# One row of an output projection on eight DMA engines, A's projection in four pieces, and eight tiny matmuls at the start

## The chip, the cores and the metric

The kernel runs on one core of one Trainium2 chip. The metric is the device time of one execution in microseconds (us). A kernel is told by the median of its runs, and two kernels are compared by runs of the same rounds on the same chip. A difference under 2% is called "same".

Some words used below: PE is the matrix engine, DVE and ACT are the vector and scalar engines, SP is the engine that issues the loads. A matmul on PE comes with a weight load, recorded apart (2328 of each in the kernel before). Sixteen DMA engines move the data; the packets that one of them moves, one behind the other, are called its stream, and the 4-byte packet with which it reports its part of a load as done is its semaphore packet. Between the packets of the loads, in the same streams, stand packets of two queues that the profile calls "instruction" (in the kernel before six of 16,384 bytes on q8, and from 1.0 us on two of 8,192 on q14); such a packet is taken to bring a block of an engine's program and is called a fetch, one of 8,192 bytes a half fetch. A stand is a time in which PE is idle in the middle of its work although it waits for no semaphore ("issue" in the profile).

## The reference

There are two attention layers with one query each, A and B. They differ only in how much of the cache they see: A the last 2048 of 8192 positions, B all.

```python
B, Sq, D = 1, 1, 576
Hq, Hkv, Sk, Dh = 32, 16, 8192, 128
W = min(4096, max(256, Sk // 4))                       # 2048, A only
q = (x @ wq).reshape(B, Sq, Hq, Dh)...                  # transposed to heads
k = jnp.repeat(k_cache[:, :, Sk - W:, :], rep, axis=1)  # B: the whole cache
v = jnp.repeat(v_cache[:, :, Sk - W:, :], rep, axis=1)
p = softmax(einsum("bhqd,bhkd->bhqk", q, k) * Dh ** -0.5)
o = einsum("bhqk,bhkd->bhqd", p, v)
return o.transpose(...).reshape(B, Sq, Hq * Dh) @ wo    # wo: 4096 x 576
out = concatenate([a, b], axis=-1)
```

The last step is what the change touches: a row of 4096 numbers times `wo`. The kernel puts 32 rows of `wo` on each of 128 partitions ("row 31" is the last of them on every partition), so the product is 32 steps of a 128-deep matmul.

## The kernel before

After five rounds of caches (one for A, four for B) the kernel loads both `wo` into the buffers of the K and V cache as these come free, then multiplies. A's product is in two pieces of 288 columns (64 matmuls), B's in four of 144 (128 matmuls).

```python
OUTS = [2, 4]
# ... (setup, loads of K and V, transposes, scores, softmax, sums over V)

    def load_wo(P, lo, n, off, res):
        load(slots[:, off:off + n * DM], lambda: wos[P].rearrange("(p j) n -> p (j n)", p=128)[:, lo * DM:(lo + n) * DM],
             res, "wo%d_%d" % (P, lo))

    def wo_part(P, lo, n, off, res):
        def mm(pe):
            for jj in range(lo, lo + n):
                w = DM // OUTS[P]
                for j in range(OUTS[P]):
                    o = off + (jj - lo) * DM + j % 2 * (DM // 2) + j // 2 * w
                    at = jj + j % 2 * 31
                    ins = pe.matmul(ktps[P + j // 2][32 * j:32 * j + 32, 0:w], lhsT=opj[:, P, at:at + 32],
                                    rhs=slots[:, o:o + w], start=(jj == 0), stop=(jj == HQ - 1))
            return ins
        add("pe", mm, reads=[("opj", P)] + res, writes=[("bank", P + k) for k in range(P + 1)])

# ...
    wo_loads = [
        (0, 0, 32, 0, [("k", 0), ("k", 1, 0)]),
        (1, 0, 21, WQ_W, [("k", 1, 1)]),
        (1, 21, 7, 2 * SLOT, [("v", 0), ("v", 1)]),
        (1, 28, 3, 2 * SLOT + 7 * DM, [("w", 0)]),
        (1, 31, 1, 2 * SLOT + 10 * DM, [("w", 1)])]
    for P, lo, n, off, res in wo_loads:
        load_wo(P, lo, n, off, res)
    combine([NG - 1])          # B's last four matmuls that gather the heads
    o_columns(1)
    for P in range(2):
        for Q, lo, n, off, res in wo_loads:
            if Q == P:
                wo_part(P, lo, n, off, res)
        finish_out(P)
```

## Time and profile before

| what | before |
|---|---|
| time, median (lowest to highest) | 245.43 us (245.33 to 245.59), 3 runs |
| span of the profiled execution | 243.8 us |
| A's product starts / ends | 232.7 / 236.8 us |
| B's first part starts, after its weights | 238.29 us |
| last load landed / last matmul ended | 241.94 / 242.26 us |
| 16 KiB instruction fetches (queue q8), start | 38.03, 50.50, 65.08, 71.18, 236.06, 240.13 us |

The profile's page is read from the engine shares to the DMA slices and queues, then the chain of work that ended last, then the timeline of the tail. Those lines, and how packets were put to streams, are shown in the prediction. "Last landing" is the last semaphore packet of the last load plus the time until its update is seen (0.44 us here).

### The profile page before, as it was taken

The page shows a single profiled execution, that of the slowest core. Times are in us where ns is not written, and L with a number is a line of the kernel's source. Part 1 is how long each engine was busy: PE and PEld are TensorE (multiplying, and loading weights), DVE is VectorE, ACT ScalarE, POOL GpSimd, SP SyncE. Part 2 cuts the span into 40 slices and gives each one's busy share as a digit, 9 for nine tenths or more (in the row PEclk, how much of TensorE's full clock was granted, in tenths as well). Part 3 has the DMA queues.
Part 4 walks back from the last instruction along what each step waited for, and adds up shares of the span by engine and source line. Part 5 has one row for each costly group of instructions (what it writes and reads, how often), then busy time and mean ns, then how long its engine had stood idle before and what let it go on. Part 6 is the DMA issues. An engine that isn't in the chain of part 4 may idle for free. (4 is left out here: it accounts for less than half of the span.)

```text
span 243.8 us, 5220 instructions
## 1 busy us (share of the span) xinstructions
PE 164.1 (67%) x2328; PEld 119.3 (49%) x2328; DVE 88.3 (36%) x152; ACT 92.9 (38%) x96; POOL 6.8 (3%) x34
## 2 busy tenths in 40 slices
PE   0060739984387995393999472999458699746864
PEld 0020239762236773233978231987233677535753
DVE  0100126874207454203455222456321355532120
ACT  2000016876006686101677400678600387630000
POOL 6001000000000000000000000000000000000000
PEclk9996557999569999566799959799956799955899
DMA  8999999999999999899999999999989999989994
GB/s 323 452 454 396 430 430 427 425 425 430 446 427 426 489 398 462 371 430 436 495 399 462 403 409 430 430 489 419 452 382 436 436 489 398 484 376 411 422 405 177
DMA packets 4112, 102.88 MB, mean 422 GB/s; under 512 B 516, under 2 KB 648, under 8 KB 904
## 3 DMA queue, kind: packets, MB, share of 16 engines
q1 hardware_dynamic: 4040, 102.76, 98.3%
q8 instruction: 6, 0.10, 0.2%
q10 hardware_dynamic: 64, 0.00, 0.0%
q14 instruction: 2, 0.02, 0.0%
HBM read 102.76 MB, written 0.00 MB: 422 GB/s over the span
## 5 line engine op out<-in xcount | busy, mean ns | idle before, releaser
L510 ACT ACTIVATE kt<-ktps 128x1024 bf16<-128x1024 bf16 x80 | 79.4, 1038 | 86.9 <-PE ktps L500 86.9
L500 PE MATMUL ktps<-ident,slots 128*128 128x128 bf16 x1280 | 85.9, 231 | 18.9 <-PEq L214 18.2
L500 PEld LDWEIGHTS ktps<-ident,slots 128*128 128x128 bf16 x1280 | 79.9, 104 | 34.3 <-issue 34.3
L513 DVE COPY kt<-ktps 128x1024 bf16<-128x1024 bf16 x80 | 60.8, 770 | 53.3 <-PE ktps L500 53.3
L592 PE MATMUL opsum<-slots,ptm 128*32 128x512 bf16 x320 | 27.1, 511 | 12.4 <-PEq L214 12.4
L525 PE MATMUL sacc<-kt,qst 128*32 128x512 bf16 x320 | 25.4, 392 | 2.2 <-PEq L214 2.2
L592 PEld LDWEIGHTS opsum<-slots,ptm 128*32 128x32 bf16 x320 | 13.1, 123 | 25.1 <-issue 22.9
L563 PE MATMUL misc<-ident,psb 128*128 128x128 bf16 x40 | 5.1, 307 | 15.8 <-PEq L214 15.8
L610 DVE TENSOR_TENSOR vtmp<-opsum,maskV 128x512 f32<-128x512 f32 x4 | 2.8, 692 | 32.3 <-PE opsum L592 32.3
L551 ACT ACTIVATE psb<-sacc,stat 128x2048 bf16<-128x2048 f32 x5 | 9.8, 1967 | 9.7 <-DVE stat L540 9.7
L563 PEld LDWEIGHTS misc<-ident,psb 128*128 128x128 bf16 x40 | 3.9, 138 | 18.3 <-issue 18.3
L570 DVE TENSOR_TENSOR ptm<-misc,maskP 128x1024 bf16<-128x1024 bf16 x5 | 3.5, 692 | 16.4 <-PE misc L563 16.4
L525 PEld LDWEIGHTS sacc<-kt,qst 128*32 128x32 bf16 x320 | 5.0, 94 | 8.2 <-issue 4.6
L695 PE MATMUL ktps<-slots,opj 128*32 128x144 bf16 (+1 forms) x192 | 6.8, 247 | 2.7 <-DMA slots<-in_B_wo_dram 2.7
L707 ACT ACTIVATE outsb<-ktps 64x144 bf16<-64x144 f32 x1 | 0.3, 288 | 21.5 <-PE ktps L695 21.5
L460 PE MATMUL turned<-slots,xpad 128*32 128x512 bf16 x36 | 4.0, 631 | 6.4 <-DMA slots<-in_B_wq_dram 6.4
L475 DVE CAST qcol<-misc 128x32 bf16<-128x32 f32 x2 | 0.6, 300 | 19.8 <-PE misc L471 19.8
L695 PEld LDWEIGHTS ktps<-slots,opj 128*32 128x32 bf16 x192 | 5.2, 97 | 4.1 <-DMA slots<-in_B_wo_dram 3.6
L460 PE MATMUL opsum<-slots,xpad 128*32 128x512 bf16 x36 | 3.5, 559 | 5.2 <-DMA slots<-in_A_wq_dram 5.2
L485 POOL COPY qst<-qcol 128x32 bf16<-128x32 bf16 x8 | 1.7, 213 | 153.1 <-PE sacc L525 153.1
L441 PE MATMUL misc<-xnine,twice 16*128 16x18 bf16 x4 | 0.3, 171 | 8.0 <-DMA xnine<-in_B_x_dram 8.0
L466 ACT ACTIVATE qrow<-opsum 128x512 bf16<-128x512 f32 x1 | 0.6, 598 | 12.8 <-PE opsum L460 12.8
(77 smaller groups left out, 57.0 us busy)
## 6 DMA issues: line engine op xcount, KB each, us to landing
slots<-in_B_k_cache_dram SPq DMA_DIRECT2D x8, 4096.0 KB
slots<-in_A_k_cache_dram SPq DMA_DIRECT2D x4, 2048.0 KB
slots<-in_A_v_cache_dram SPq DMA_DIRECT2D x4, 2048.0 KB
slots<-in_B_wq_dram SPq DMA_DIRECT2D x1, 4608.0 KB, 23.1
slots<-in_A_wo_dram SPq DMA_DIRECT2D x1, 4608.0 KB, 20.0
slots<-in_A_wq_dram SPq DMA_DIRECT2D x1, 3072.0 KB, 12.6
slots<-in_B_wo_dram SPq DMA_DIRECT2D x1, 3024.0 KB, 27.1
slots<-in_A_wq_dram SPq DMA_DIRECT2D x1, 1536.0 KB, 6.2
```

Source lines behind the costliest of these rows:

```text
L460: ins = pe.matmul((turned if P else opsum)[32 * j:32 * j + 32, :], lhsT=xpad[:, P, u, :], rhs=slots[:, o:o + 512], start=(u == 0), stop=(u ...
L485: return pool.tensor_copy(dst, src)
L500: ins = pe.matmul(ktps_bf[q][:, t * 128:(t + 1) * 128], lhsT=slots[:, o:o + 128], rhs=ident[:, :], start=True, stop=True, is_transpose=True)
L510: add("act", lambda act, src=src, dst=dst: act.activation(dst, src, ACT.Copy), reads=[("bank", q)], writes=[("kt", u % NKT, q)], tag="e%d% ...
L513: add("dve", lambda dve, src=src, dst=dst: dve.tensor_copy(dst, src), reads=[("bank", q)], writes=[("kt", u % NKT, q)], tag="e%d%d" % (u, q))
L525: ins = pe.matmul(sacc[32 * j:32 * j + 32, :], lhsT=qst[:, o:o + 32], rhs=rhs, start=(u == 0 and e == 0), stop=True, skip_group_check=True)
L551: return act.activation(dst, src, ACT.Exp, bias=st(C_NB + g), scale=SCALE, accum_out=st(C_L + g))
L563: ins = pe.matmul(dst[:, t * 128:(t + 1) * 128], lhsT=psb[:, o:o + 128], rhs=ident[:, :], start=True, stop=True, is_transpose=True)
L570: return dve.tensor_tensor(ptm[:, c * 1024:(c + 1) * 1024].rearrange("p (t y) -> p t y", t=8), dst.rearrange("p (t y) -> p t y", t=8), mas ...
L592: ins = pe.matmul(opsum[64 * j + 32 * x:64 * j + 32 * x + 32, :], lhsT=ptm[:, o:o + 32], rhs=v[:, at[0], at[1], :, :, b:b + 128], start=(n ...
L610: add("dve", lambda dve: dve.tensor_tensor(vtmp[:, :, :], src, by, ALU.mult), reads=[B_O, w], writes=["vtmp"], tag="keep")
L695: ins = pe.matmul(ktps[P + j // 2][32 * j:32 * j + 32, 0:w], lhsT=opj[:, P, at:at + 32], rhs=slots[:, o:o + w], start=(jj == 0), stop=(jj ...
```

## The change

The streams of the sixteen DMA engines don't end together (their last semaphores came at 239.52 to 241.50 us in the kernel before), and the last load waits for the latest. The intent, as far as the change shows it, is to move a little work from the late streams to the early ones. A's row 31 is taken off the load that all sixteen carry and is loaded by eight engines only (four rows on each of partitions 0 to 31). The product is rearranged accordingly (sixteen matmuls that are 32 deep, from a weight tile `opjR`), A's result is made in four pieces as B's is, and eight tiny matmuls are put at the start of PE's program.

```diff
+    def warm_up(pe):
+        for k in range(8):
+            ins = pe.matmul(misc[0:32, 400:401], lhsT=ident[:, 0:32], rhs=ident[:, 0:1], start=True, stop=True)
+        return ins
+    add("pe", warm_up, reads=["ident"], writes=[B_M])
 ... (cut: opjR is allocated and zeroed)
+    def wo_row(pe, P, weights, jj, row, start, stop):
+        for j in range(4):                                   # A too: four pieces of 144 columns
+            w, o, at = DM // 4, j % 2 * (DM // 2) + j // 2 * (DM // 4), jj + j % 2 * 31
+            ins = pe.matmul(ktps[2 * P + j // 2][32 * j:32 * j + 32, 0:w], lhsT=weights[:, at:at + 32],
+                            rhs=row[:, o:o + w], start=start, stop=stop)
+        return ins
+    def last_column():
+        for j in range(4):
+            add("dve", lambda dve, j=j: dve.tensor_copy(opjR[:, 31 + j:32 + j], wsum[32 * j:32 * j + 32, 303:304]), ...)
+    def load_last():
+        for i in range(4):
+            def src(i=i):
+                return wos[0].rearrange("(j e i r) n -> r i e j n", j=4, e=8, i=4)[31, i]
+            dst = bass.AP(tensor=slots, offset=(4 * SLOT) * i + 31 * DM, ap=[[4 * 4 * SLOT, 8], [DM, 4], [1, DM]])
+            add("sp", lambda sp, dst=dst, src=src: sp.dma_start(dst, src()), writes=[("last", i)], dma="last", ...)
+    def wo_last():
+        def mm(pe):
+            for j in range(4):
+                ins = wo_row(pe, 0, opjR[:, :], j, slots[0:32, (31 + j) * DM:(32 + j) * DM], False, j == 3)
+            return ins
+        add("pe", mm, ...)
 ... (cut: finish_out makes both results in two halves, one by DVE and one by ACT)
     wo_loads = [
-        (0, 0, 32, 0, [("k", 0), ("k", 1, 0)]),
-        (1, 0, 21, WQ_W, [("k", 1, 1)]),
+        (0, 0, 31, 0, [("k", 0), ("k", 1, 0)]),
+        (1, 0, 21, 35 * DM, [("k", 1, 1)]),
 ...
         load_wo(P, lo, n, off, res)
+        if P == 0:
+            load_last()
```

More of the change, by code (lines that the diff above doesn't have):

```diff
@@ L21 @@
 WQ_W = 18432
-OUTS = [2, 4]
 class Op:
@@ L338, in bass_concat_heads__sliding_block_cached__gqa_block_cached__decode_kernel @@
     accs = nc.alloc_sbuf_tensor("accs", [128, NG, DH], F32)
+    opjR = nc.alloc_sbuf_tensor("opjR", [32, 96], BF16)
     opj = nc.alloc_sbuf_tensor("opj", [128, 2, 96], BF16)
@@ L373, in setup @@
     def setup(pool):
-        for t in (ident, twice, xpad, selq, warm, identf, pick, pickB, qst):
+        for t in (ident, twice, opjR, xpad, selq, warm, identf, pick, pickB, qst):
             pool.memset(t[:], 0.0)
@@ L377, in setup @@
         return pool.memset(opj[:], 0.0)
-    add("pool", setup, writes=["ident", "twice0", ("xpad", 0), ("xpad", 1), "selq", "ones", "warm", "identf", "pick", "pickB",
+    add("pool", setup, writes=["ident", "twice0", "opjR0", ("xpad", 0), ("xpad", 1), "selq", "ones", "warm", "identf", "pick", "pickB",
                                ("qst", 0), ("qst", 1), ("opj", 0), ("opj", 1)])
@@ L690, in mm @@
             for jj in range(lo, lo + n):
-                w = DM // OUTS[P]
-                for j in range(OUTS[P]):
-                    o = off + (jj - lo) * DM + j % 2 * (DM // 2) + j // 2 * w
-                    at = jj + j % 2 * 31
-                    ins = pe.matmul(ktps[P + j // 2][32 * j:32 * j + 32, 0:w], lhsT=opj[:, P, at:at + 32],
-                                    rhs=slots[:, o:o + w], start=(jj == 0), stop=(jj == HQ - 1))
-            return ins
-        add("pe", mm, reads=[("opj", P)] + res, writes=[("bank", P + k) for k in range(P + 1)])
+                ins = wo_row(pe, P, opj[:, P, :], jj, slots[:, off + (jj - lo) * DM:off + (jj - lo + 1) * DM],
+                             jj == 0, P == 1 and jj == HQ - 1)
@@ new lines, in mm @@
+            return ins
+        add("pe", mm, reads=[("opj", P)] + res, writes=[("bank", 2 * P), ("bank", 2 * P + 1)])
+    def wo_row(pe, P, weights, jj, row, start, stop):
[6 more added lines that the diff above has]
+        for j in range(4):
+            add("dve", lambda dve, j=j: dve.tensor_copy(opjR[:, 31 + j:32 + j], wsum[32 * j:32 * j + 32, 303:304]),
+                reads=[B_W, "opjR0"], writes=[("opjR", j)])
@@ new lines, in load_last @@
+    def load_last():
[3 more added lines that the diff above has]
+            dst = bass.AP(tensor=slots, offset=(4 * SLOT) * i + 31 * DM, ap=[[4 * 4 * SLOT, 8], [DM, 4], [1, DM]])
+            add("sp", lambda sp, dst=dst, src=src: sp.dma_start(dst, src()), writes=[("last", i)], dma="last",
+                after=[("k", 1, 0), ("k", 1, 1)])
+    def wo_last():
[3 more added lines that the diff above has]
+            return ins
+        add("pe", mm, reads=[("opjR", j) for j in range(4)] + [("last", j) for j in range(4)], writes=[("bank", 0), ("bank", 1)])
@@ L702, in finish_out @@
     def finish_out(P):
-        w = DM // OUTS[P]
-        for k, name in enumerate(("dve", "act")[0:P + 1]):
-            dst, src = outsb[0:64, P, k * w:(k + 1) * w], ktps[P + k][64 * k:64 * k + 64, 0:w]
+        w = DM // 4
+        for k, name in enumerate(("dve", "act")):
+            dst, src = outsb[0:64, P, k * w:(k + 1) * w], ktps[2 * P + k][64 * k:64 * k + 64, 0:w]
             add(name, lambda eng, k=k, dst=dst, src=src:
                 eng.activation(dst, src, ACT.Copy) if k else eng.tensor_copy(dst, src),
-                reads=[("bank", P + k)], writes=[("outsb", P, k)]).key = ("outsb", P)
+                reads=[("bank", 2 * P + k)], writes=[("outsb", P, k)]).key = ("outsb", P)
@@ L709, in finish_out @@
         add("sp", lambda sp: sp.dma_start(out[0, 0:1, P * DM:(P + 1) * DM].rearrange("o (j n) -> (o j) n", j=2),
                                           outsb[31:33, P, :]),
-            reads=[("outsb", P, k) for k in range(P + 1)], writes=[("out", P)], dma="out%d" % P)
+            reads=[("outsb", P, 0), ("outsb", P, 1)], writes=[("out", P)], dma="out%d" % P)
     WQ = [(4 * SLOT - WQ_W, [("v", 2)]), (SLOT, [("k", 1, 0), ("k", 1, 1), ("v", 0)])]
@@ L772, in bass_concat_heads__sliding_block_cached__gqa_block_cached__decode_kernel @@
             o_columns(0)
+            last_column()
         v_sums(g)
@@ L789, in bass_concat_heads__sliding_block_cached__gqa_block_cached__decode_kernel @@
                 wo_part(P, lo, n, off, res)
+        if P == 0:
+            wo_last()
         finish_out(P)
```

## The prediction

> **What bounds the kernel now.** I read the page's engine shares first, then the slices of DMA and the queues, then the chain of waits at the end, then the timeline of the last 15 us, and last the trace's single records of DMA packets.
>
> The page of the kernel before (engine shares, DMA rows of the 40 slices, queues, bytes):
>
> ```profile
> PE 164.1 (67%) x2328; PEld 119.3 (49%) x2328; DVE 88.3 (36%) x152; ACT 92.9 (38%) x96; POOL 6.8 (3%) x34
> ...
> DMA  8999999999999999899999999999989999989994
> ...
> q1 hardware_dynamic: 4040, 102.76, 98.3%
> q8 instruction: 6, 0.10, 0.2%
> ...
> q14 instruction: 2, 0.02, 0.0%
> HBM read 102.76 MB, written 0.00 MB: 422 GB/s over the span
> ```
>
> No compute engine is above 67%, while the DMA engines are at 8 or 9 tenths in every slice but the last. The loads (q1) alone fill 98.3% of sixteen engines' span. So the kernel is a stream of 102.76 MB with a short tail, and only two things can move the end: fewer or better spread bytes, and what follows the last byte. The two "instruction" queues fetch the engines' own programs through the same DMA engines; they look negligible at 0.2%, and they are what this change is about.
>
> The chain of waits, its end (start us, us, what):
>
> ```profile
> 226.53 4.20 PE opsum L592 x61
> 230.73 0.02 issue
> 230.75 0.33 SPq L398
> 231.08 0.04 issue
> 231.12 10.45 DMA slots<-in_B_wo_dram
> 241.57 0.04 issue
> 241.62 0.64 PE ktps L695 x16
> 242.26 0.02 issue
> 242.28 0.30 DVE outsb L707
> ```
>
> The transfer of 10.45 us is not slow: it holds 432 KB and queues behind loads issued earlier (A's wo at 210.80, B's at 211.18 and 231.1). After the last landing come only 16 matmuls, one eviction and the store, about 2 us that the change does not touch.
>
> The timeline, output products (start us, us, what):
>
> ```profile
> 232.84 3.97 PE L695 MATMUL ktps<-slots,opj 128*32 128x288 bf16 x62
> ...
> 236.85 0.45 DVE L707 CAST outsb<-ktps 64x288 bf16<-64x288 f32 x1 [3.62 <-PE ktps L695]
> ...
> 238.29 1.50 PE L695 MATMUL ktps<-slots,opj 128*32 128x144 bf16 x84 [1.48 <-DMA slots<-in_B_wo_dram]
> 240.59 0.62 PE L695 MATMUL ktps<-slots,opj 128*32 128x144 bf16 x28 [0.81 <-DMA slots<-in_B_wo_dram]
> ```
>
> A's product ends at 236.8 and PE then waits for B's weights until 238.29: A's product is off the path, with 1.5 us to spare.
>
> The packet records settle the rest. Within one DMA engine the next packet starts 3 or 4 ns before the one before it ends, so all sixteen engines' streams can be followed from 1.0 us to their end. No stream has a gap. They do not end together: the 4-byte semaphore packets of the last load (B's row 31) come at 239.52 to 240.08 us on nine streams, 240.26 and 240.76 on two, and 241.14, 241.26, 241.30, 241.37 and 241.50 on five. Those seven streams are exactly those that carried an instruction fetch: the five have a 16,384-byte packet (at 38.03, 50.50, 65.08, 71.18 and 236.06 us, 1.02 to 1.07 us each, and the load packet after it is longer too, 1.15 us instead of 0.61 after the first), the two an 8,192-byte packet. The sixth 16,384-byte packet, at 240.13, follows no running stream: it fell on an engine that was done, and cost nothing. The kernel ends with the slowest of the five, although the mean of the sixteen semaphores is 240.4, about 1.1 us earlier.
>
> [...]
>
> **The change, part by part.**
>
> 1. *A's load of 31 rows instead of 32 on 128 partitions.* Each engine moves eight packets of 35,712 bytes instead of 36,864. A 36,864-byte packet takes 1.366 us (seven in 219.07 to 228.63), so a packet saves 1.366 x 1152/36864 = 0.043 us and each of the 16 engines 0.34 us.
> 2. *Row 31 as four DMAs of 8 x 4 rows.* Engines 0 to 7 get 16 packets of 1152 bytes and four semaphores each. A 1152-byte packet took 0.051 us in the tail, a semaphore 0.009: 0.82 + 0.04 = 0.85 us. Net: engines 0 to 7 become 0.85 - 0.34 = 0.51 us longer, engines 8 to 15 0.34 us shorter.
> 3. *A's product in four pieces.* 124 + 16 matmuls of 144 columns instead of 64 of 288. The 84 that B ran back to back took 1.50 us, 0.018 each: 140 x 0.018 = 2.5 us against 4.1 now, done near 235.3. Its eviction is split over two engines. All that lies in the slack before 238.29: worth nothing. The 16 matmuls of row 31 wait for loads that stand directly behind A's in the queue and land near 231, before PE starts on them.
> 4. *Four copies of one column on DVE* after A's cast at 226.57: DVE idles 4.0 us before 230.76, so nothing. Bank 3, now also B's, was last read at 233.0, long before B starts. Four more issues on SP come at 211, when the stream has 9 us of V queued.
> 5. *Eight tiny matmuls at the start and 76 more in the tail.* At two instructions each PE's program grows by 168[...]. A further fetch comes in the tail[...]. About 1.07 us on one engine. On a stream that would end at 240.1 it gives 241.2 at most before the shifts of step 2, so it need not be the last.
>
> Sum, if the fetches lie on engines 8 to 15: the last semaphore moves from 241.50 to 241.16; engines 0 to 7 end by 240.08 + 0.51 = 240.6, or 240.8 with the half fetch at 240.26. The end moves by -0.34 us: 245.43 - 0.34 = 245.1.
>
> **The rivals.**
>
> *One of the five late streams is among engines 0 to 7.* Then it gains 0.51 us and ends at 241.65 to 242.0: the time becomes 245.6 to 245.9. For it: nothing in the trace names the engines; if blocks 2 to 6 went to engines 2 to 6 everything seen would look the same. Against it: the change puts work on engines 0 to 7 on purpose, which makes sense only if the late ones are the others, and the two streams that stored A's result[...] have no 16 KiB fetch, only one half fetch.
>
> *The eighth block spoils it.* If the new fetch falls on a stream that already carries one (the half one at 240.76, less 0.34, plus 1.07 = 241.5), the end stays where it is: 245.4. If the mapping of blocks to engines depends on their number, a fetch can land on engines 0 to 7 on top of row 31: 240.08 + 0.51 + 1.07 = 241.66, and the time is 245.6.
>
> *A's quicker product.* A rival only in name: PE would still wait for B's weights; zero.
>
> **Range and chances.** I give the intended case 60%, no effect 15%, a loss of 0.2 to 0.5 us 25%. The middle of that is about -0.2 us: I predict 245.2, and take 244.8 to 245.9 as the range, whose ends are the two cases with 0.1 to 0.3 us for runs that differ (the three of before spread over 0.26 us). Two per cent is 4.9 us; nothing found here is larger than 2.0 us, the whole spread of the last semaphores, so "within" gets 0.985.
>
> **What would show it.** In the packet records after: 16 packets of 1152 bytes on eight streams and none on eight; the order of the last semaphores; late streams among the eight without row 31 (right) or with it (wrong). The gap before B's first product should stay, and A's should end near 235. The last load should land near 241.2 rather than 241.57. Seven or more q8 packets should show the eighth block, one of them near 238. The prediction is wrong at its root if the streams show gaps, that is if SP's new issues or waits starve the queue, or if the packets of 1152 bytes from scattered rows of the weights take much more than 0.051 us.

The sum: the last semaphore from 241.50 to 241.16, so -0.34 us, and 245.43 - 0.34 = 245.1; part 5 put nothing into it. For "engines 0 to 7" in part 2, the trace of the changed kernel shows eight streams with 16 packets of row 31 each, and no numbers. The "eighth block" of part 5 is one more fetch near 238 us, for the 168 instructions that PE's program grows by; that it would come was the assumption, and six packets were seen on q8 before and after.

## The result, and the profile after

| | before | changed |
|---|---|---|
| median of 6 runs each, same rounds | 245.45 us | 246.84 us |
| lowest to highest | 245.33 to 245.59 | 246.02 to 247.79 |
| span of the profiled execution | 243.8 | 245.5 |
| last load landed | 241.94 | 242.29 |
| last matmul ended | 242.26 | 243.97 |

The ratio is 1.0055, 95% interval 1.0034 to 1.0077: "same" by the 2% rule, but a loss of 1.4 us and outside the predicted range. A ratio here and below is the mean time of one kernel's fast runs over the mean of the other's in the same rounds, without the profiled run of the later kernels, so it isn't quite the ratio of the medians quoted. Every kernel told of below gave correct results.

The page of the changed kernel, the same rows as shown for the kernel before:

```profile
PE 166.4 (68%) x2412; PEld 121.4 (49%) x2412; DVE 88.6 (36%) x156; ACT 93.0 (38%) x97; POOL 6.9 (3%) x35
...
DMA  8998999999999999999999999999999999999991
...
q1 hardware_dynamic: 4200, 102.76, 97.7%
q8 instruction: 6, 0.10, 0.2%
...
q14 instruction: 3, 0.02, 0.0%
HBM read 102.76 MB, written 0.00 MB: 419 GB/s over the span
```

The bytes are the same and q1 has 160 packets more. PE has 84 matmuls more: 76 of the products and the eight tiny ones. The last DMA slice fell from 4 to 1: a larger part of that last slice (6.1 us) now passes without loads, so something else ends the kernel. The predicted sign of the longer program, a seventh packet on q8, isn't there; there are six as before. The one more on q14 is a 96-byte packet at 0.10 us, not a fetch of a block.

The end of the chain of waits (start us, us, what):

```profile
233.80 0.34 PE ktps L681 x5
...
234.21 2.26 PE ktps L706 x127
236.47 3.48 issue
239.95 4.02 PE ktps L706 x133
243.97 0.02 issue
244.00 0.30 DVE outsb L738
```

In the kernel before, this chain held 10.45 us of DMA. Now it has no DMA in it: PE does A's product, stands for 3.48 us marked "issue", which is time in which it waited for no semaphore that the profile shows, and then runs without a break to the end.

The timeline of PE, same kernel (start us, us, what, and in brackets the idle time before it):

```profile
234.08 2.10 PE L706 MATMUL ktps<-slots,opj 128*32 128x144 bf16 x118
236.11 0.36 PE L706 MATMUL ktps<-slots,opjR 32*32 32x144 bf16 x11
239.95 0.33 PE L706 MATMUL ktps<-slots,opjR 32*32 32x144 bf16 x5 [3.48 <-issue]
240.21 3.72 PE L706 MATMUL ktps<-slots,opj 128*32 128x144 bf16 x128
```

The stand falls inside A's row 31, after eleven of its sixteen matmuls: the data and weights of both sides are the same, so no load and no engine can be what PE waits for. Counted from the end of the program, 268 recorded PE instructions (matmuls, weight loads and three semaphore waits) are left. In three runs below PE stands at two places, and these are 256 recorded instructions apart each time (268 and 12 from the end in whole_stall, 296 and 40 in split_w22, 308 and 52 in split_nostall); I take 256 as the length of a block. Then 268 is one block and 12 more. The packet records have a 16,384-byte packet of q8 from 237.36 to 238.42, and PE goes on at 239.95, 1.53 us after its end. So the stand is PE waiting for a block of its own program: 0.9 us until the packet begins, 1.06 us for the packet, 1.5 us until PE runs.

B's weights had landed at 238.48, so from there on the stand was lost time: 1.5 us. Then B's 128 matmuls took 3.72 us. Here are the windows of the changed kernel, A's product and B's, and after them B's first 84 matmuls in the kernel before (columns in the first line):

```profile
core 0: us, PE busy (x) PEld busy (x) DVE busy (x) ACT busy (x) POOL busy (x), PEclk, DMA share, GB/s
234.10:236.10 2.00, 2.00 (x129) 1.89 (x119) 0.19 (x1) 0.00 (x0) 0.00 (x0) 1.00 0.92 395
240.21:243.47 3.26, 3.26 (x113) 3.26 (x116) 0.30 (x1) 0.29 (x1) 0.00 (x0) 0.50 0.16 57
```

```profile
238.29:239.79 1.50, 1.50 (x84) 1.31 (x84) 0.00 (x0) 0.00 (x0) 0.00 (x0) 1.00 0.96 387
```

The granted clock was 1.00 in A's product and 0.50 in B's: from start to start one matmul took 30.0 ns there, and 15.6 ns once the clock was back at 243.47. The half clock lasted from 240.06 to 243.47, 3413 ns. The clock records of this trace and of the kernel before hold two levels, 1.0 and 0.5, and each piece but the last of a trace lasts 3413 ns or a whole multiple of it. The 3413 ns ahead of the half clock (236.65 to 240.06) lie almost wholly in the stand (236.47 to 239.95). That a stand brings the half clock on isn't shown by this trace alone.

The loads, for their part: the last semaphores are at 241.82 and 241.66 us on two of the eight streams that carry row 31 (their fetches were at 37.72 and 52.85), and at 240.91, 240.96 and 241.09 on three of the others (fetches at 69.94, 237.36 and 62.85). Before, the five were at 241.14 to 241.50. No stream has a gap.

This gives the sum of the loss in this execution: the last landing came 0.35 us later (242.29 for 241.94). With the 0.32 us of matmuls that followed it before, PE would have ended at 242.61. It ended at 243.97, so 1.36 us come from the stand together with the half clock. Together they make 1.71, the whole difference of the spans (1.7).

### The profile page after: what moved, and what is told of

Read it like the earlier page. It is cut to its first block, busy times and chain, and to the rows that moved or that the text cites. A ratio compares the mean times of both kernels' runs of the same rounds, so it can differ in the third digit from the quotient of the medians.

```text
span 245.5 us, 5398 instructions
## 1 busy us (share of the span) xinstructions
PE 166.4 (68%) x2412; PEld 121.4 (49%) x2412; DVE 88.6 (36%) x156; ACT 93.0 (38%) x97; POOL 6.9 (3%) x35
## 5 line engine op out<-in xcount | busy, mean ns | idle before, releaser
L506 PE MATMUL ktps<-ident,slots 128*128 128x128 bf16 x1280 | 86.8, 232 | 22.5 <-PEq L213 18.2
L598 PE MATMUL opsum<-slots,ptm 128*32 128x512 bf16 x320 | 27.9, 523 | 8.2 <-PEq L213 8.2
L598 PEld LDWEIGHTS opsum<-slots,ptm 128*32 128x32 bf16 x320 | 13.7, 127 | 20.9 <-issue 18.5
L466 PE MATMUL opsum<-slots,xpad 128*32 128x512 bf16 x36 | 4.0, 630 | 5.6 <-DMA slots<-in_A_wq_dram 5.6
L706 PE MATMUL ktps<-slots,opj 128*32 128x144 bf16 x252 | 5.9, 269 | 0.0
L569 PE MATMUL turned<-ident,psb 128*128 128x128 bf16 x40 | 5.3, 313 | 0.0
```

The source lines that it names most:

```text
L466: ins = pe.matmul((turned if P else opsum)[32 * j:32 * j + 32, :], lhsT=xpad[:, P, u, :], rhs=slots[:, o:o + 512], start=(u == 0), stop=(u ...
L506: ins = pe.matmul(ktps_bf[q][:, t * 128:(t + 1) * 128], lhsT=slots[:, o:o + 128], rhs=ident[:, :], start=True, stop=True, is_transpose=True)
L569: ins = pe.matmul(dst[:, t * 128:(t + 1) * 128], lhsT=psb[:, o:o + 128], rhs=ident[:, :], start=True, stop=True, is_transpose=True)
L598: ins = pe.matmul(opsum[64 * j + 32 * x:64 * j + 32 * x + 32, :], lhsT=ptm[:, o:o + 32], rhs=v[:, at[0], at[1], :, :, b:b + 128], start=(n ...
L706: ins = pe.matmul(ktps[2 * P + j // 2][32 * j:32 * j + 32, 0:w], lhsT=weights[:, at:at + 32], rhs=row[:, o:o + w], start=start, stop=stop)
```

## The experiments

My theory after the traces: the loss comes from PE waiting for a block of its program, with the half clock after it, and about 0.3 us hide underneath, because two of the five late streams are among the eight that carry row 31. The rivals: (1) only the late streams matter and the stand is a matter of the profiled run; (2) the four-piece product or the added loads cost of themselves; (3) the stand costs only because B is half clocked, or only because the streams are late.

### Longer programs: another twenty tiny matmuls

If the stand is a block boundary, its place moves with the number of instructions ahead of it. The change with 28 tiny matmuls has its boundary well inside A's product.

```diff
     def warm_up(pe):
-        for k in range(8):
+        for k in range(28):
```

> The changed kernel with 28 instead of 8 tiny matmuls at the start of PE's program, so that the program's block boundary moves 40 instructions towards the beginning[...]. Theory A (the lost 1.4 us are mostly a wait for instructions on PE, followed by a catch-up at half clock, and the rest, 0.3 to 0.4 us, is row 31 on late engines): no idle stretch of PE labelled issue between A's and B's product, and 245.7 to 246.0 us, ratio 1.001 to 1.002. Rival B (the instruction wait is hidden by the wait for B's weights, and it is the unbalanced loads that cost): 246.5 us or more, ratio 1.004 or more.

Measured: 245.63 us (245.50 to 245.83), ratio to the kernel before 1.0017 (1.0003 to 1.0031). A loss of 1.4 us became one of 0.4 although PE has more to do. The timeline of PE:

```profile
236.48 0.43 PE L706 MATMUL ktps<-slots,opjR 32*32 32x144 bf16 x16
237.96 1.50 PE L706 MATMUL ktps<-slots,opj 128*32 128x144 bf16 x84 [1.05 <-DMA slots<-in_B_wo_dram]
240.44 0.49 PE L706 MATMUL ktps<-slots,opj 128*32 128x144 bf16 x19 [0.98 <-DMA slots<-in_B_wo_dram]
241.72 0.88 PE L706 MATMUL ktps<-slots,opj 128*32 128x144 bf16 x25 [0.79 <-issue]
```

A's row 31 now runs through, and PE waits for B's weights as in the kernel before. A smaller stand of 0.79 us came at 240.93, before the last 25 matmuls, behind a fetch at 239.12. It cost nothing here: the last loads landed only at 241.95 and 242.31, and the last sixteen matmuls, begun at 241.99 and 242.35, waited for them. All five early fetches lay on streams without row 31, which nobody had asked for: the tiny matmuls also changed which streams carry fetches. But the sixth, of 239.12, fell on a stream with row 31, and that stream ended last, at 241.82 (241.50 before). That is what is left of the loss in this trace.

### The whole row 31 with the same program lengths

Here row 31 is loaded with the others on sixteen engines, A stays in four pieces, and the number of tiny matmuls makes the program as long as the changed one (20), or as the one with 28 (40).

```diff
-        for k in range(8):
+        for k in range(20):      # whole_nostall: 40
...
-        (0, 0, 31, 0, [("k", 0), ("k", 1, 0)]),
+        (0, 0, 32, 0, [("k", 0), ("k", 1, 0)]),
...
-        if P == 0:
-            load_last()
```

> A in four pieces as in the change, but its row 31 loaded with the other rows on all 16 engines; 20 tiny matmuls at the start so that the program is as long as the changed one and the block boundary falls at the same distance from its end. Theory A: PE again idles 3 us or more just before B's product, and the time is 245.9 to 246.8 with a wider spread than the 0.3 us of before, ratio 1.002 to 1.006. Rival B (only the row's loads cost): 245.4, ratio 1.000.

> As the run before, but 40 tiny matmuls at the start, so that the boundary lies 40 instructions earlier. Neither cause is left: theory A expects 245.3 to 245.6, ratio 0.999 to 1.001, and no idle stretch of PE labelled issue of over 1 us in the tail. Rival C (A's product in four pieces itself costs[...]): 245.8 or more.

Measured: 245.40 us (ratio 1.0007, 0.9994 to 1.0021) with 20, and 245.43 (1.0012, 0.9998 to 1.0026) with 40. The first was to show the stand again and didn't: PE stood 0.81 us at the same place, 268 from the end, and that was over before B's weights came. (It stood again, 0.51 us, at 12 from the end, one block of 256 further. All loads had landed by 241.85 and PE went on at 242.41, so in the traced execution, 245.62 us, this second stand set the end.) Its block had been fetched from 234.17, when PE was still 183 recorded instructions ahead of the boundary, whereas in the changed kernel the packet began only when PE already stood. So the length of the program alone doesn't decide; when the fetch comes does. What the two runs do show is that A in four pieces costs nothing of itself, which speaks against rival 2 for that part.

### Which engine gets which block

The packet records carry no engine. To name them, fourteen tiny loads were added, on 2, 3, ... 15 partitions. If a load on few partitions runs on some of the engines that one on more partitions uses, the number of tiny packets on a stream gives its place in a row. This place is what is called the engine's number here: 15 minus the count, and 0 or 1 for a count of 14. In the first try they were issued early.

```diff
+            for n in range(2, 16):
+                add("act", lambda act, n=n: act.dma_start(tagt[0:n, n - 2, :], wqs[0][0:n, 0:64]),
+                    reads=["qrow"], writes=[("tag", n)], dma="tag")
```

> The kernel before with fourteen tiny extra loads, on 2, 3, ... 15 partitions of 128 bytes each, issued from ACT between the two query products. If a load on n partitions runs on the n lowest-numbered engines, the number of such packets on a stream gives its engine's number. Theory A (late streams are partly among engines 0 to 7): the five late streams of the kernel before get numbers on both sides of 8. Rival B (they are all in 8 to 15, and the changed program's eighth block moved them): all five have numbers of 8 or more. The result must be right and the time within 0.3% of before.

Measured: 246.17 us against 245.26, 0.37% more. From 27 us on some streams had gaps around the tiny loads (near 28 us, packets were in flight on as few as 11 of the 16), so packets couldn't be followed over that place: inconclusive. The second try issued them from SP right behind A's `wo` load, where the queue is full, and ran twice to see whether the same program gives the same engines.

```diff
         load_wo(P, lo, n, off, res)
+        if P == 0:
+            for m in range(2, 16):
+                add("sp", lambda sp, m=m: sp.dma_start(tagt[0:m, m - 2, :], wqs[0][0:m, 0:64]), writes=[("tag", m)], dma="tag")
```

> The kernel before with fourteen tiny loads behind A's wo in the same queue, on 2, 3, ... 15 partitions: the first numbering run put them between the two query products, where they made the streams run dry and they could not be followed. The count of 128-byte packets on a stream numbers its engine (15 minus the number, 14 for both 0 and 1). Theory A (which block goes to which engine is not tied to one half): the five late streams have numbers on both sides of 8. Rival B: all have 8 or more. Time within 0.5% of before.

> The same program once more. If a block's engine is fixed by the program (theory F), every fetch falls on the same engine number as in the run before; if the fetches go round the engines from one execution to the next (theory R), the numbers are shifted by the same amount for all blocks.

Measured (246.28 and 246.51 us; the tiny loads cost about 1 us, so the times aren't compared): in both executions the 16 KiB fetches of about 38, 52, 60, 69 and 237 us fell on engines 5, 6, 9, 10 and 11, and the half fetches on engine 3 and on 0 or 1. The sixteen streams carried 0, 1, 2, ... 13 tiny packets once each and 14 twice, so the row is complete but for the order of 0 and 1. For this text the placing was the same twice, and it is two below eight and three above. The 60% case of the prediction, all five above, was wrong already for the kernel before.

The same numbering was put into the changed kernel, with 8 and with 28 tiny matmuls:

> The changed kernel with the numbering loads. In its profile the first two fetches fell on streams with row 31 and the next three on streams without. Theory F expects that again; theory R expects neighbouring numbers with another start. The idle stretch of PE before B's product should be there again, 3 us or more.

> The variant of the change without the instruction wait (28 tiny matmuls at the start), with the numbering loads. In its profile all five late streams were among the eight without row 31. Theory F expects that again, with the same pattern (five fetches on engines 8 to 15, the sixth below 8); theory R allows any other set of neighbours.

Measured: num_after 246.68 us, with fetches at 38, 52, 62 and 70 us on engines 5, 6, 9 and 10, the one of 237 us on an engine of 8 or above, and the stand again (3.47 us, half clock from 239.29). This fits the reading of the streams with row 31 as engines 0 to 7: in the first trace of the changed kernel the fetches of 37.72 and 52.85 were on such streams, and those of 62.85, 69.94 and 237.36 on others. num_split 246.74 us: the fetches at 28.6 and 79.8 us on engines 10 and 14 and one of those between, at 53.6 or 72.8, on 13. All five were probably above 7, but the row's loads came late and some streams couldn't be followed with certainty past 228.4 us. So twenty tiny matmuls more move the first fetch from 38 to 28.6 us and all five to other engines.

### The number of tiny matmuls: 0, 4, 12 and 22

Four kernels differ from the changed one only in that number (0 leaves the function out).

> The changed kernel without the eight tiny matmuls, so that the block boundaries move 16 instructions later: the last one before B falls 4 instructions into B's product instead of 12 ahead of it[...]. Theory A (PE waits for a block[...]): PE still stands for the block until about 240, now at the start of B's product, and the time is 246.0 to 247.5, ratio 1.003 to 1.008, with a spread of 1 us or more. Rival E (the tiny matmuls at the start did the harm): at or below 245.7.

> The changed kernel with 4 instead of 8 tiny matmuls: the block boundary that PE stood at lies 260 instructions from the program's end, 4 ahead of B's product. Theory A (standing for the block and catching up at half clock makes the loss beyond row 31): as with 8, PE stands 3 us or more, resumes between 239 and 240.5, and the time is 246.0 to 247.8, ratio 1.003 to 1.007. If the place of the boundary is not what counts (rival P: something that only the exact text with 8 has), 245.5 to 245.9 as without the stand.

> The changed kernel with 12 tiny matmuls: the boundary lies 276 instructions from the end, 20 ahead of B's product, and the crossing before it 23 instructions behind PE's wait at the start of the tail. Theory A: the same stand of 3 us or more and 246.0 to 247.8, ratio 1.003 to 1.007. If the crossing is near enough to the wait[...] (as with 22, at 3 instructions), the stand is 1 us or less and the time 245.4 to 246.2.

> The changed kernel with 22 tiny matmuls: the block boundary that is crossed in the tail moves to 3 instructions behind PE's wait at the start of the tail[...]. The program stays as many blocks long as the changed one, so the fetches should fall on the same engines. Theory A: the wait for instructions shrinks to 1 us or less and is over before B's weights land; what stays is row 31 on late engines: 245.5 to 245.9, ratio 1.001 to 1.002. Rival G (the cure in the run with 28 was that the fetches went to other engines): 246.5 or more.

Measured, together with the changed kernel (8) and the one of 28. The boundary is counted in recorded PE instructions before the end of the program; "packet" is the start of the q8 packet for it, and the row of 28 is left open where that block came early. "Below engine 8" means that the stream carries row 31's packets; only the five fetches that came before the tail's last one are counted:

| tiny matmuls | boundary | packet, us | PE stands there, us | five late fetches below engine 8 | median us (range) | ratio (95%) |
|---|---|---|---|---|---|---|
| 0 | 252 | 236.49 | 0.3, after 2.9 on B's weights | 2 | 245.79 (245.46-247.41) | 1.0029 (1.0008-1.0051) |
| 4 | 260 | 238.32 | 3.4 | 2 | 246.98 (245.60-248.04) | 1.0059 (1.0035-1.0084) |
| 8, changed | 268 | 237.36 | 3.5 | 2 | 246.84 (246.02-247.79) | 1.0055 (1.0034-1.0077) |
| 12 | 276 | 238.54 | 3.4 | 0 | 246.72 (246.23-247.92) | 1.0056 (1.0039-1.0072) |
| 22 | 296 | 233.94 | 0.3; then 1.3 at 40 from the end | 0 | 245.92 (245.39-246.25) | 1.0018 (1.0006-1.0030) |
| 28 | 308 | early | none; then 0.8 at 52 from the end | 0; the sixth is | 245.63 (245.50-245.83) | 1.0017 (1.0003-1.0031) |

The boundary moves by two instructions (a matmul and its weight load) for each tiny matmul, exactly: 252, 260, 268, 276, 296. The second stands, 40 and 52 from the end with 22 and 28 tiny matmuls, and 12 with the whole row, lie 256 behind 296, 308 and 268. That settles that the stand is at a fixed place of the program, a block boundary, and not at a matmul that waits for something. The time follows the stand: with 4, 8 and 12 about 246.8 (one of the six runs with 4 was at 245.60), with 22 and 28 under 246. With 4 and 12, PE went on at 240.90 and 240.91; for 4, up to 240.5 had been expected. With none, PE is already waiting for B's weights when it meets the boundary three matmuls into B, so most of the fetch is hidden, and the expectation of 246.0 or more mostly missed; one run of six was at 247.41.

The decisive one is 12, as its five late fetches all lie on streams without row 31. Its DMA balance is the one that the change intended: the last semaphore came at 241.39, earlier than the 241.50 of the kernel before. Still it lost 1.4 us in the medians. The timeline of PE with 12:

```profile
237.24 0.30 PE L706 MATMUL ktps<-slots,opjR 32*32 32x144 bf16 x7
240.91 0.34 PE L706 MATMUL ktps<-slots,opjR 32*32 32x144 bf16 x9 [3.37 <-issue]
241.18 3.82 PE L706 MATMUL ktps<-slots,opj 128*32 128x144 bf16 x128
```

The stand is there, now with nine matmuls of A left instead of five, and B again takes 3.8 us at half clock (241.37 to 244.79). So the stand costs its 1.4 us with good streams too: the first rival falls, and so does that part of the third that needs late streams.

This trace is of an execution of 247.92 us, the slowest with 12. What sets such a time can be read from the five traces with a stand over 3 us: from A's first matmul to the end of the last one is 9.9 to 10.2 us in all five, and A's product began at 233.55, 233.62, 233.96, 234.94 and 235.09 us in executions of 246.59, 246.68, 246.86, 247.78 and 247.92. The loads no longer set the end, so every delay ahead of A's product comes out in the time. In the kernel before it began at 232.71, with 1.5 us to spare before B's weights.

That the stand costs only by way of the half clock remains possible, as no run here has a stand over 3 us at full clock.

With 4, 8 and 12, why is the fetch late? In the traces with 0, 4, 8 and 12 (six, with the repeats of 8) the packet starts 3.2 to 3.45 us after PE has passed the instruction 254 before the boundary, and with 4 to 12 A's product covers these 254 in 2.2 us. With 22 the packet starts at 233.94, when PE is 236 recorded instructions ahead of the boundary:

```profile
236.29 0.24 PE L706 MATMUL ktps<-slots,opj 128*32 128x144 bf16 x3 [0.25 <-issue]
...
242.43 0.49 PE L706 MATMUL ktps<-slots,opj 128*32 128x144 bf16 x19 [1.29 <-issue]
```

and almost nothing is lost there. But PE stands a second time, for 1.29 us, at the next boundary, 1.43 us past the end of the fetch of 240.00. The last load landed at 242.18, and with the 0.32 us of matmuls behind it PE would have ended at 242.50. It ended at 242.95 (242.26 in the kernel before), so most of what 22 still loses in this trace is the second stand, and not row 31 on late engines, as the expectation had it. The expectation also took the fetches to stay on the same engines; they didn't, so rival G is answered by the run with 12, not by this one.

Where the packet came early, another thing differs too. With 22 and in the whole-row kernel the block ahead of the boundary, counted as 256 recorded instructions, begins about 3 and 7 recorded instructions behind the 1.8 us for which PE waits on the DVE sums before A's product, and with 0 to 12 it begins 22 to 47 behind it. No rule is shown by this: the traces don't show when a fetch is asked for, and in the changed kernel the next fetch (241.18) came only 1.2 us after PE had passed the boundary (239.95).

### Only the loads

Here A is left in two pieces and there are no tiny matmuls; only row 31 is loaded by eight engines. This separates the DMA part from PE's program.

```diff
-    def warm_up(pe): ...
...
-        for j in range(4):
-            w, o, at = DM // 4, j % 2 * (DM // 2) + j // 2 * (DM // 4), jj + j % 2 * 31
+        for j in range(OUTS[P]):          # OUTS = [2, 4]
+            w = DM // OUTS[P]
+            o, at = j % 2 * (DM // 2) + j // 2 * w, jj + j % 2 * 31
```

> Only the loads of the change: row 31 as four rows on partitions 0 to 31, A's product in two pieces as before, no tiny matmuls. Theory A: the last semaphore on an engine below 8 moves by +0.3 to +0.5 us, the time to 245.6 to 245.9, ratio 1.001 to 1.002. Rival H (the loads are harmless and the four pieces cost all): 1.000. The prediction on record had -0.34 us for its likeliest case.

Measured: 245.57 us (245.38 to 245.67) against 245.33, ratio 1.0008 (0.9995 to 1.0021). Two late streams carry row 31 and end at 241.78 and 241.89. The end of its chain of waits:

```profile
232.75 9.26 DMA slots<-in_B_wo_dram
242.01 0.04 issue
242.05 0.63 PE ktps L703 x16
```

As in the kernel before, the last two loads and 16 matmuls end it, begun 0.43 us later than the 241.62 of before. So the row by itself costs about 0.2 us in the medians, just below the 245.6 to 245.9 expected; the interval doesn't exclude zero.

To see the row's own cost, its four loads were issued a second time into a buffer that is no longer used.

```diff
+        for i in range(4):
+            dst2 = bass.AP(tensor=kt, offset=(NKT * UNIT) * i, ap=[[4 * NKT * UNIT, 8], [DM, 4], [1, DM]])
+            add("sp", lambda sp, dst2=dst2, src2=src2: sp.dma_start(dst2, src2()), writes=[("again", i)], dma="again", ...)
```

> As the run before, with the four loads of row 31 issued once more into a tile that nobody reads any more: 0.85 us more for each engine from 0 to 7. Theory A (the end is set by the last of the engines): 0.85 us above the run before, 246.4 to 246.8, ratio 1.0045 to 1.0055. If the engines were not the limit: less than half of that.

Measured: 246.34 us, with the late streams of the eight at 242.57 and 242.78. That is 0.77 over split_two in the medians, and 0.79 and 0.89 at the two semaphores, where the prediction had 0.85. So that term holds in the traces and the upper runs. But the five runs fell into two groups: 246.42, 246.34, 246.34 and 245.65, 245.62, and with the lower ones the ratio is 1.0026 (1.0013 to 1.0039), below the 1.0045 to 1.0055 expected. Three looks at the same text were to catch the lower group:

> The run with the doubled loads of row 31 once more, for its trace: its five times fell in two groups, 245.6 and 246.4 us. Theory M (from one execution to the next the blocks of PE's program fall on other engines): an execution of 245.6 us has all its late streams among the engines 8 to 15, or fewer of them; one of 246.4 us has a full fetch on at least one engine below 8, as the first trace had (38 and 50 us). Rival N (the fetches stay where they are and the time differs for another reason, such as the clock of PE or a wait): both groups show the same engines.

> The same again, with the same two theories; among three traces at least one of each group of times is likely, as two of five times were in the lower group.

> The same a third time, with the same two theories: the engines of the fetches (below 8 or not) against the time of this execution, 245.6 or 246.4 us.

Measured: 246.17, 246.10 and 246.44 us, all of the upper kind, with the row's late streams ending at 242.4 to 242.7 (in the first, two streams could not be told apart with certainty). The lower group was never in a trace, so its cause stays open.

### The changed kernel once more

> The changed kernel again, for a second trace without numbering loads. Theory A: PE stands still at the same instruction, 268 from its end, until about 1.5 us after the end of a fetch that starts at 236 us or later, and the time exceeds 245.8 us by as much as that block comes later than B's weights, plus what the half clock costs, if it is granted then. Rival N2: no such stand, and the time still above 246.

Measured: 246.59 us, a stand of 3.50 us at the same instruction (PE goes on at 239.56, the packet began at 237.12), half clock from 239.91 to 243.33, two late streams below engine 8. With num_after that makes three of three traces of this arrangement with the stand.

None of these kernels is faster than the kernel before. The kernel with 12 has all late streams above 7, and its last semaphore came at 241.39 against 241.50 before: without the stand some 0.1 us would be left to gain.

## Why the prediction was wrong

**What bounds the kernel, and parts 1 and 2: right.** Loads with no gap, and the late streams are those with a fetch. The late streams above 7 came about 0.35 us earlier (0.34 predicted). The last landing came 0.35 us later, where 0.51 on a late stream that had not been the very last was predicted (241.65 to 242.0 for the rival, measured 241.82). The row doubled cost 0.77 to 0.89 where 0.85 was said. (As the packets overlap by 3 to 4 ns, one adds 0.047 us to its stream and a semaphore 0.006, so the prediction's own readings give 0.78.) One reading was off without harm to the sum: 241.57 is the landing of rows 28 to 30, after which twelve matmuls run; row 31, the last load, landed at 241.94, ahead of the last four.

**The choice that all five late streams are engines 8 to 15: wrong.** It was given 60% on the ground that the change "makes sense only if the late ones are the others". The numbering showed 5, 6, 9, 10 and 11, and the two half fetches below 8. (With the half fetch of the stream that ended at 240.76 below 8 too, the prediction's own sum gives 240.76 + 0.51 = 241.27 even in its likeliest case, not 241.16.) An intent of whoever wrote the change isn't evidence; the records fitted both equally well, as the prediction itself said. The first rival came true for the loads, and alone it gives 245.57 (split_two), inside the range.

**Part 5, the eighth block: the step that failed.** It counted a fetch as about 1.07 us of load on one stream and asked only on which stream it would fall. That PE itself can't go on without the block was never put in. Measured: 0.9 us before the packet, 1.06 us for it and 1.5 us after it, a stand of 3.5 us in which PE was one block short of the end. It also had the wrong fetch in view. It asked about the one of 240.13, whose successor came at 241.18. By the stands seen, block boundaries lie 256 apart, and the kernel before is 168 instructions shorter, so the boundary 268 from the end of the changed kernel is the one 100 from the end of the kernel before. That block came at 236.06, and PE reached it at 239.49, inside B's product and behind the wait for B's weights; there it cost PE nothing. By this count the change put it ahead of that wait. The sign given, more than six packets on q8, didn't show; the count of packets says nothing about where the boundaries lie.

**Part 3, A's product in four pieces "in the slack, worth nothing": wrong in its consequence.** The product took about 2.3 us, the stand left aside, as worked out (2.5). But with 280 instructions instead of 128 it is longer than a block, and it runs through one in 2.2 us at full clock, less than the 3.2 to 3.45 us after which the packet of the next one even started in six traces. The slack before B's weights, 1.5 us, was smaller than the stand. That the four pieces cost nothing of themselves is shown by the whole-row kernels (245.40 and 245.43, intervals that include no difference).

**The half clock: not in the prediction at all.** B's 128 matmuls would take 2.2 us at full clock (1.50 for the 84 of the kernel before and 44 more at 15.6 ns), and took 3.72, 1.5 us more. Without it the stand would have let B end at about 239.95 + 0.26 + 2.2 = 242.4, just inside the 242.61 that the loads allow; that is worked out, not run. So by this estimate the loss needs both in the changed kernel. The half clock alone cost nothing: in the whole-row kernel with 40, B's product began in time, at 238.16, ran at half clock from 238.59 to 242.00, and ended at 242.30. All five traces with a stand over 3 us have the half clock right behind it. Three others have it too, with longest idle gaps of only 2.1 to 2.9 us: the kernel with no tiny matmuls, the whole-row one with 40, and the second numbering of the kernel before. In each of the eight, the 3413 ns ahead of the half clock had PE's matmuls idle for at least 2.1 us (2.08 in the second numbering, from 236.09 to 239.50). In num_split 1.9 us of the 3413 ns from 237.90 to 241.31 were idle, in the kernel before 1.9 us of those from 237.18 to 240.59, its most idle such stretch between A's product and the last load, and in both the clock stayed at 1.0. This fits the stand as the cause, but no run takes the stand alone and holds the clock.

**What stays open.** What fixes a block's engine: texts whose first fetch is near 38 us have two of five below 8, those with 12 or more tiny matmuls and a first fetch near 28 us none, as far as followed. When a fetch is asked for. The two groups of split_two_double. Why the start of A's product moves by 1.5 us from execution to execution; that it does is why kernels with the stand spread over 1.7 us or more, and the kernel before over 0.3, as far as five traces show it.

## What to carry to other kernels

Count PE's recorded instructions (a matmul is two) between its last waits and the end. Here 254 of them ran in 2.2 us, the packet of the next block began 3.2 to 3.45 us after the first of them, PE went on 1.3 to 1.5 us after the packet's end, and in five traces it stood 3.4 to 3.5 us. "Issue" idle in the middle of one product, at a place that moves by two for each matmul added ahead, is how it looked. The fetches also delayed the loads: one took 1.02 to 1.07 us in its stream, and in the kernel before the five streams with one ended 1.1 to 2.0 us after the nine without. Work "in the slack" was not free here, where it made PE run through its program faster (280 instructions in about 2.3 us, where 128 had taken 4.1). And before a load is moved between engines on the strength of who is late, have the engines numbered by a run, as the packets of a profile don't name them.
